# Eighteen loads of x behind the last store of an FFT and gated-cosine kernel

## The chip, the core and the metric

The kernel runs on one core of a Trainium2 chip. The metric is the time of one execution on the device in microseconds (us). TensorE (PE) multiplies matrices, VectorE (DVE), ScalarE (ACT) and GpSimd (POOL) work on elements, SyncE (SP) issues most DMAs, and 16 DMA engines move the data between DRAM and SBUF, the memory of 128 partitions on the core. A DMA that SP or ACT issues is split over these engines; it tells its end by a semaphore, on which whatever needs the data waits.

## The reference

Two stages. The first is the real part of a Fourier transform of x over sequence and channel; the second is a two-layer network with the gate h cos(h).

```
x: (8, 3008, 256) float32;  w_in: (256, 2048);  w_out: (2048, 256)
X = np.fft.fft(np.fft.fft(x, axis=1), axis=2).real.astype(np.float32)
x = X.reshape(24064, 256)
h = x @ w_in
g = h * np.cos(h)
out = (g @ w_out).astype(np.float32)
```

## The kernel before

The 3008 positions of a sequence are written as 47 x 64: `x_r` is x seen as (batch, s2, s1, channel) with 47 values of s2 and 64 of s1. One s2 is 64 rows of 1 KB that lie next to each other in DRAM, so that `x_r[b, r0:r0+k, i0:i1]` is k pieces of (i1 - i0) KB, 64 KB apart. The transform goes in two halves (`first_half`, `second_half`) with a turn through DRAM in between (`store_z`, `load_z`); the second stage takes the result in steps of 256 columns and two blocks of 128 hidden channels (`mm1`, `act_e`, `dve_h`, `act_round`, `dve_frac`, `act_sin`, `dve_g`, `dve_s`, `mm2`), and its results go out through `store_out`.

Two SBUF tiles of 128 partitions x 4096 floats, `xs[0]` and `xs[1]` (tile name `xp` in the profile), hold the part of x that is being worked on. For the first batch `load_x` fills them (line 194): rows s2 of 0 to 31 go to partitions 32, 34, ... 94, those of 31 to 46 to partitions 0, 2, ... 30, and the mirrored positions, read backwards, go to the odd partitions in the same places. The descriptors, one for each piece that a DMA engine moves, are cut to 1 KB by `max_dma_last_dim=1024`. For later batches `load_later_x` (line 180) loads them in groups of at most seven rows, and `fold_rows` on POOL (line 325) and `middle_later` on PE (line 350) read them.

Other loads and stores that the prediction uses: the first matrix in `load_w` (lines 226 and 232, 128 partitions, 2 KB pieces), the second in `load_w2` (line 244, two DMAs of 512 KB in 1 KB pieces one right after the other), the intermediate in `load_z` (line 511), and in `second_half` a row of 1 KB that SP stores to DRAM (line 545) and spreads back over the partitions with the next DMA (line 546), which reads what the first one wrote.

The order of the work is written by hand: `tc.manual_schedule()` keeps the instructions of each engine and each queue in the order of the calls, and the framework adds the semaphore waits that the reads and writes of the tiles ask for. A loop over the steps `t` calls every stage; in its last turn it calls `combine_last`, which forms the last results and stores them in two halves of four DMAs each with `store_last` (line 906), on SP, ACT and one on POOL, and then leaves the loop. Nothing follows but the closing of the program (line 1149 in the profile).

Of the kernel before, what the change touches and what calls it, by code (L numbers as in the profile page):

```python
# [18 lines left out]
ND = 256  # L19
# [115 lines left out]
def kernel(  # L135
# [930 lines left out]
    for t in range(LAG, n + LAG + 1):  # L1066
# [55 lines left out]
        for call in todo.pop(t, ()):  # L1122
            call[0](*call[1:])


# [1 line left out]
_INS = ['x', 'moe_w_in', 'moe_w_out']  # L1127
# [26 lines left out]
```

## Time and profile before

| | |
|---|---|
| median of 2 runs | 1933.53 us (1933.52 to 1933.53) |
| the profiled execution, its own time | 1935.07 us |
| its span, first to last instruction | 1933.3 us |
| mean granted TensorE clock | 0.998 |
| busy share of PE, DVE, ACT, POOL | 99%, 92%, 79%, 21% |
| moved by the DMA engines | 89.16 MB, a mean of 46 GB/s |
| last reads of `xs[0]` and `xs[1]` by POOL (line 325) | begin at 1623.3 us |
| last four stores on SP (line 906) | 1927.49 to 1930.09 us |

All times inside the execution are from the start of the span. The profile shows one execution; its own time is that of the same execution with what lies around the span. An engine's busy share counts its instructions, not the issuing of DMAs; what SP, ACT and POOL issue stands in rows marked with a q behind the engine (SPq) or with the operation DMA_DIRECT2D. The rows named DMA and GB/s cut a stretch of time into 40 equal slices: the first gives the mean busy share of the 16 DMA engines in tenths, the second what they moved.

### The profile page before, as it was taken

To read this page: it belongs to the slowest core of one execution; us is meant where nothing else is said; L and a number is where in the kernel's file an instruction comes from. 1 tells how busy PE (TensorE), PEld (TensorE's weight loads), DVE (VectorE), ACT (ScalarE), POOL (GpSimd) and SP (SyncE) were. 2 spreads that over 40 slices of the span, in tenths; PEclk is the share of its full clock that TensorE was granted. 3 is DMA by queue.
4 is the path that set the end of the run, shared out by engine and by line. 5 is a ranking of instruction groups with operands and counts; after the bars stand their busy time and mean duration, and the time that the engine had idled before them with its cause. 6 is when DMAs were issued, how large, how long until landed. Compare 5 with 4: busy or idle time off the path is not lost.

```text
span 1933.3 us, 30495 instructions
## 1 busy us (share of the span) xinstructions
PE 1919.4 (99%) x9520; PEld 1690.2 (87%) x9520; DVE 1778.9 (92%) x3338; ACT 1527.8 (79%) x2870; POOL 413.5 (21%) x494
## 2 busy tenths in 40 slices
PE   9999999999999999999999999999999999999998
PEld 5888899888998889988898888988889888898887
DVE  5999989999899998999989999999999999999998
ACT  4787888788788887888877887788877888788775
POOL 5322112221122211222112221122211222111111
PEclk9999999999999999999999999999999999999999
DMA  7311220012111121112211022110131000110000
GB/s 201 108 54 43 76 55 24 22 47 76 47 25 26 46 81 38 27 25 55 78 31 31 21 56 83 29 26 24 53 85 31 25 20 24 55 28 10 12 22 23
DMA packets 160215, 89.16 MB, mean 46 GB/s; under 512 B 108039, under 2 KB 154910, under 8 KB 157713
## 3 DMA queue, kind: packets, MB, share of 16 engines
q1 hardware_dynamic: 158653, 85.58, 16.6%
q8 instruction: 76, 1.25, 0.3%
q0 software_dynamic: 896, 1.07, 0.2%
q14 instruction: 86, 0.70, 0.1%
q10 hardware_dynamic: 504, 0.56, 0.1%
HBM read 49.88 MB, written 37.28 MB: 45 GB/s over the span
## 4 chain that ended last, share of the span: by engine, by line
PE 96%; DMA 2%; SPq 1%; DVE 1%; issue 0%; POOL 0%; ACT 0%; ACTq 0%; DVEq 0%; POOLq 0%
PE M L812 58%; PE H L721 33%; PE pb L525 2%; PE pz L419 2%; DMA w<-in_moe_w_out_dram 1%; DMA xp<-in_x_dram 1%; SPq L194 0%; POOL VX L864 0%; PE pz L453 0%; DMA zd<-zs 0%; PE pz L350 0%; PE M L419 0%; SPq L502 0%; DMA out_dram<-ob 0%; DMA xz<-in_x_dram 0%
## 5 line engine op out<-in xcount | busy, mean ns | idle before, releaser
L812 PE MATMUL M<-S,VX 128*128 128x256 f32 (+1 forms) x2304 | 612.6, 375 | 0.0
L812 PEld LDWEIGHTS M<-S,VX 128*128 128x128 f32 x2304 | 438.3, 190 | 49.4
L752 ACT ACTIVATE r<-H 128x512 f32<-128x512 f32 (+1 forms) x384 | 226.0, 589 | 262.9 <-DVE h L737 261.6
L762 ACT ACTIVATE r<-r 128x1024 f32<-128x1024 f32 (+1 forms) x384 | 394.8, 1028 | 21.3 <-DVE r L756 15.8
L721 PE MATMUL H<-pq,WC 128*128 128x256 f32 (+1 forms) x1536 | 393.8, 379 | 0.7 <-ACT H L691 0.7
L721 PE MATMUL H<-pq,WS 128*128 128x256 f32 (+1 forms) x1536 | 388.3, 375 | 1.7 <-ACT ew L732 1.5
L812 PE MATMUL M<-r,w 128*128 128x256 f32 (+1 forms) x1536 | 387.9, 375 | 0.0
L691 ACT ACTIVATE H<-nb,wn 128x256 f32<-128x256 f32 (+1 forms) x762 | 360.6, 473 | 16.2 <-DMA wn<-wd 2.4
L737 DVE TENSOR_TENSOR h<-ew,H 128x512 f32<-128x512 f32 (+1 forms) x384 | 258.6, 673 | 99.7 <-PE H L721 64.1
L721 PEld LDWEIGHTS H<-pq,WC 128*128 128x128 f32 x1536 | 283.7, 190 | 49.8 <-ACT r L752 16.2
L812 PEld LDWEIGHTS M<-r,w 128*128 128x128 f32 x1536 | 300.5, 196 | 27.1
L721 PEld LDWEIGHTS H<-pq,WS 128*128 128x128 f32 x1536 | 291.6, 190 | 36.0 <-ACT ew L732 3.2
L756 DVE SCALAR_TENSOR_TENSOR r<-r,H 128x512 f32<-128x512 f32 (+1 forms) x384 | 258.7, 674 | 25.4 <-ACT r L752 9.1
L864 POOL TENSOR_TENSOR cb<-cb,mr 128x256 f32<-128x256 f32 (+3 forms) x190 | 159.6, 850 | 523.1 <-DVE S L787 484.0
L732 ACT ACTIVATE ew<-H 128x512 f32<-128x512 f32 (+1 forms) x384 | 225.6, 587 | 54.3 <-PE H L721 45.4
L756 DVE SCALAR_TENSOR_TENSOR r<-r,h 128x512 f32<-128x512 f32 (+1 forms) x384 | 259.4, 675 | 0.0
L777 DVE TENSOR_TENSOR S<-r 128x512 f32<-128x512 f32 (+1 forms) x384 | 258.8, 674 | 0.1
L766 DVE SCALAR_TENSOR_TENSOR r<-h,r 128x512 f32<-128x512 f32 (+1 forms) x384 | 258.0, 672 | 0.0
L766 DVE SCALAR_TENSOR_TENSOR r<-H,r 128x512 f32<-128x512 f32 (+1 forms) x384 | 255.8, 666 | 2.3 <-ACT r L762 1.7
L752 ACT ACTIVATE r<-h 128x512 f32<-128x512 f32 (+1 forms) x384 | 235.9, 614 | 0.0
L812 PE MATMUL M<-S,w 128*128 128x256 f32 (+1 forms) x768 | 226.1, 376 | 1.5 <-DVE S L787 1.5
L325 POOL TENSOR_TENSOR xs<-xp 113x512 f32<-113x512 f32 x112 | 142.9, 1276 | 387.2 <-DVE S L787 387.2
(106 smaller groups left out, 1587.8 us busy)
## 6 DMA issues: line engine op xcount, KB each, us to landing
out_dram<-ob SPq DMA_DIRECT2D x726, 32.0 KB
xp<-in_x_dram SPq DMA_DIRECT2D x256, 56.0 KB
z<-zd SPq DMA_DIRECT2D x8, 1280.0 KB
zd<-zs SPq DMA_DIRECT2D x224, 40.0 KB
nb<-nd SPq DMA_DIRECT2D x39, 128.0 KB
zd<-zs SPq DMA_DIRECT2D x224, 8.0 KB
xp<-in_x_dram SPq DMA_DIRECT2D x52, 48.0 KB
xp<-in_x_dram SPq DMA_DIRECT2D x42, 49.0 KB
```

Source lines behind the costliest of these rows:

```text
L325: return nc.gpsimd.tensor_tensor(out=xs2[e][0:XL], in0=xv[:, 0], in1=xv[:, 1], op=ALU.subtract if e else ALU.add,)
L691: nc.scalar.activation(out=s.H[:, u * T : u * T + T], in_=s.nb[:, 0:T], func=AF.Copy, bias=0.25, scale=wn[:, f : f + 1],)
L721: nc.tensor.matmul(s.H[:, u * T : u * T + T], lhsT=W[:, 128 * f : 128 * f + 128], rhs=s.pq[:, e * T : e * T + T], start=False, stop=True, ...
L732: nc.scalar.mul(out=s.ew[:, 0 : 2 * s.T], in_=s.H[:, 0 : 2 * s.T], mul=2.0)
L737: return nc.vector.tensor_tensor(out=s.h[:, 0 : 2 * T].rearrange("p (u t) -> p u t", u=2)[:, :, ::-1], in0=s.ew[:, 0 : 2 * T].rearrange("p ...
L752: nc.scalar.activation(out=r, in_=h, func=AF.Copy, bias=BIG, scale=1.0)
L756: nc.vector.scalar_tensor_tensor(out=r, in0=r, scalar=-BIG, in1=h, op0=ALU.add, op1=ALU.subtract)
L762: nc.scalar.activation(out=r, in_=r, func=AF.Sin, bias=0.0, scale=SIN_SCALE)
L766: nc.vector.scalar_tensor_tensor(out=r, in0=h, scalar=-0.25, in1=r, op0=ALU.add, op1=ALU.mult)
L777: return nc.vector.tensor_tensor(out=sv[:, 0:2], in0=gv[:, 2:3].to_broadcast([128, 2, T]), in1=gv[:, 0:4:3], op=ALU.subtract,)
L812: nc.tensor.matmul(acc[key][m // 2][:, 256 * (m % 2) : 256 * (m % 2) + T], lhsT=w, rhs=a, start=first, stop=s.fp == 7, skip_group_check=True,)
L864: return nc.gpsimd.tensor_tensor(out=o, in0=a, in1=b, op=ALU.subtract if less else ALU.add)
```

## The change

Behind the loop, as the last calls of the kernel, stand DMAs that read parts of the input x (batches 1 and 2) into `xs[0]`, here named `probe`. No instruction reads them.

`tokens(pitch, size)` loads to all 128 partitions: partition p gets four rows of 1 KB from position `pitch * p` on, so that with pitch 4 the source is one piece of 512 KB and with pitch 16 pieces of 4 KB 16 KB apart. `rows(queue, p0, step, r0, k, i0, i1, size)` loads k rows of s2, 16 KB each, to the partitions p0, p0 + step, and so on; with i1 below i0 it takes the 16 positions backwards. `size` is the largest piece in bytes. All but the last call go to SP's queue; the last goes to ACT's.

```diff
+    probe = xs[0]
+
+    def rows(queue, p0, step, r0, k, i0, i1, size, to=probe):
+        n = abs(i1 - i0)
+        queue.dma_start(
+            out=to[p0 : p0 + step * k - step + 1 : step, 0 : ND * n].rearrange(
+                "r (i d) -> r i d", d=ND
+            ),
+            in_=x_r[1, r0 : r0 + k, slice(i0, i1, -1 if i1 < i0 else 1)],
+            max_dma_last_dim=size,
+        )
+
+    def tokens(pitch, size):
+        flat = x[2, 0 : 128 * pitch].rearrange("(p i) d -> p i d", i=pitch)
+        nc.sync.dma_start(
+            out=probe[:, 0 : 4 * ND].rearrange("p (i d) -> p i d", d=ND),
+            in_=flat[:, 0:4],
+            max_dma_last_dim=size,
+        )
+
+    sp, act = nc.sync, nc.scalar
+    tokens(4, 2048)
+    rows(sp, 32, 2, 0, 32, 0, 16, 1024)
+    rows(sp, 32, 2, 0, 32, 0, 16, 2048)
+    rows(sp, 32, 2, 0, 32, 0, 16, 8192)
+    rows(sp, 32, 2, 0, 32, 63, 47, 1024)
+    tokens(4, 2048)
+    tokens(16, 2048)
+    rows(sp, 0, 1, 0, 32, 0, 16, 1024)
+    rows(sp, 0, 4, 0, 32, 0, 16, 1024)
+    rows(sp, 32, 4, 0, 16, 0, 16, 1024)
+    rows(sp, 0, 1, 0, 16, 0, 16, 1024)
+    rows(sp, 0, 7, 0, 16, 0, 16, 1024)
+    for k in range(2):
+        rows(sp, 32, 2, 0, 32, 0, 16, 1024)
+        rows(sp, 33, 2, 0, 32, 63, 47, 1024)
+    rows(sp, 32, 2, 0, 32, 0, 16, 1024)
+    rows(act, 33, 2, 0, 32, 63, 47, 1024)
```

The text numbers the loads 1 to 18 in the order of these calls.

## The prediction

> **What bounds the kernel now.** I read the page first, then the end of the order of time on the engines, then the DMA rows of a few short stretches in which a load runs nearly by itself. The first lines say that TensorE sets the time from start to finish: it is busy 99% of the span, and the chain that ended last runs through the matmuls of lines 812 and 721.
>
> ```profile
> span 1933.3 us, 30495 instructions
> PE 1919.4 (99%) x9520; PEld 1690.2 (87%) x9520; DVE 1778.9 (92%) x3338; ACT 1527.8 (79%) x2870; POOL 413.5 (21%) x494
> PE 96%; DMA 2%; SPq 1%; DVE 1%; issue 0%; POOL 0%; ACT 0%; ACTq 0%; DVEq 0%; POOLq 0%
> ```
>
> None of that matters for work behind the last store: there nothing is left to hide under. What counts is the tail. The order of time for SP gives its last issues, and the view of who waited for whom on SP's queue gives the wait at the program's end (line 1149 is the closing of the program):
>
> ```profile
> 1928.75 1.34 SPq L906 DMA_DIRECT2D out_dram<-ob  x2
> ...
> SPq L1149 <- DMA out_dram<-ob: 1.8, 1, 1.8
> ```
>
> The last store is issued by 1930.09; the program then waits 1.8 us for the stores to land, to about 1931.9, and closes 1.4 us later at 1933.3. Whatever is appended starts at about 1930.1, and the closing moves with its last landing. Every microsecond of it after 1931.9 is paid in full.
>
> **What is added.** The diff issues 18 DMAs when it is counted out, 17 on SP and the last on ACT: three of 512 KB to all 128 partitions (`tokens`), twelve of 512 KB to 32 partitions and three of 256 KB to 16 partitions (`rows`). In all 15 x 0.524 + 3 x 0.262 = 8.65 MB. No engine computes, nothing is taken away, and nothing earlier moves, since the calls stand last on SP and ACT. The tile they write is read last by the folds on POOL at line 325, which end at 1624.6, so the first of them waits for nothing but its turn.
>
> **Who waits for whom.** A load that writes bytes of an earlier one must wait until that one has landed. Loads to interleaved rows need not: the twelve loads at line 194 go to even rows, odd rows and rows below 32 of one tile and are issued every 0.65 us without a wait, though they take far longer to land (the second line is of the chain that ended last: the twelfth is issued at 8.22 and has landed 9.94 us later).
>
> ```profile
> L194 SPq DMA_DIRECT2D xp<-in_x_dram x12: 609/612/772, 0.7 to 8.2; - x12
> ...
> 8.22 9.94 DMA xp<-in_x_dram
> ```
>
> So I go through the partitions. Loads 1 to 10 each overlap their predecessor and run one after the other. Load 11 (partitions 0 to 15) doesn't touch load 10 (32, 36, ... 92) and is issued right behind it. Load 12 (every seventh) meets both. The last six alternate between even and odd rows, so two are always in flight, and each waits for the one two before it. The chain has nine single steps, then 10 with 11, then 12, then three rounds of two.
>
> **The price of one step.** It has four pieces. *Hand-over*: a DMA that waits for another on the same queue starts almost at once. The 1 KB pair at lines 545 and 546 takes 283.26 to 284.35, so 1.09 us with everything in it; that is the floor of any step.
>
> ```profile
> 283.26 0.23 SPq L545 DMA_DIRECT2D nd<-pq  x1
> 284.35 0.35 SPq L546 DMA_DIRECT2D nb<-nd  x1
> ```
>
> *Issue to first packet*, from the DMA rows of two stretches. The 256 KB load of z is issued at 27.64; in the stretch 27.5 to 31 (slices of 0.0875 us) the first bytes come in the 13th slice, at 28.55: 0.9 us. The two 512 KB loads of w, cut into 1 KB pieces as most of the new loads are, are issued from 29.89; in the stretch 29.5 to 36 (slices of 0.1625 us) the stream begins at 31.6: 1.7 us.
>
> ```profile
> DMA  0000000000001568776635556400000000000009
> GB/s 0 0 0 0 0 0 0 0 0 0 0 0 70 211 234 328 304 234 187 257 141 187 211 211 234 164 24 0 0 0 0 0 23 0 0 0 0 0 0 70
> ...
> DMA  5400000069140269999999999999998677777777
> GB/s 202 151 0 0 13 0 0 0 25 76 50 25 0 57 195 347 397 384 365 384 391 384 460 347 365 359 372 340 359 347 284 208 205 199 205 214 224 218 218 217
> ```
>
> *Data.* With the queue full, the row loads of x run at 244 GB/s (6 to 18 us) and the 128-partition loads in 2 KB pieces at 404 (18 to 22); the w loads reach about 365. The lone z load needs some 1.2 us for its 262 KB, about 220 GB/s, because its engines don't start together. For 0.524 MB that is 1.3 us at 404, 1.45 at 365, 2.15 at 244.
>
> ```profile
> 6.00:18.00 12.00, 10.38 (x45) 4.45 (x43) 3.76 (x6) 1.59 (x5) 5.41 (x9) 1.00 1.03 244
> 18.00:22.00 4.00, 3.70 (x15) 1.97 (x17) 3.71 (x7) 1.94 (x6) 2.15 (x4) 0.66 1.06 404
> ```
>
> *Last packet to semaphore*: the last stores move until 1931.25 (DMA row of 1929 to 1934) and are waited for until 1931.9, 0.65 us; a load may need less, I take 0.5.
>
> **The sum.** A row load in 1 KB pieces: 1.7 + 1.85 (between 1.45 and 2.15) + 0.5 + 0.05 = 4.1. In 2 KB pieces 4.0, in 8 KB pieces 3.9, as fewer pieces should start sooner. A `tokens` load: 1.3 (between 0.9 and 1.7) + 1.55 + 0.55 = 3.4; the first 3.6, as stores are still moving; the one with gaps in the source 3.5. No row shows a load packed into rows 0 to 31, or into 0 to 15: bounds 3.8 and 6.5 (half the rate of 244), I take 5.0 for load 8 and 4.3 for load 9, which spreads over all rows. Loads 10 and 11: 0.65 until the second is issued + 2.25 + 1.7 for its data (0.7 to 2.15) = 4.6. Load 12: 3.6. The last six: with two in flight the start of one hides under the data of the other, so a round takes one step or two loads' data, 4.1 or 2 x 2.15; three rounds of 4.3 and 0.65 are 13.6.
>
> Loads 1 to 5: 3.6 + 4.1 + 4.0 + 3.9 + 4.1 = 19.7. 6 and 7: 6.9. 8 and 9: 9.3. 10 and 11: 4.6. 12: 3.6. 13 to 18: 13.6. Together 57.7, from 1930.1 on. The old wait of 1.8 goes under it, so the span grows by 55.9, from 1933.3 to 1989.2; the profiled execution, 1935.07 with what lies around its span, would show 1991. The median of the runs, 1933.53, is 1.5 lower, and with the same addition becomes **1989.4**.
>
> Bounds: with the z load's start (0.9 + 0.55) and 365 to 404 GB/s everywhere, 2.9 a row load and 2.8 a `tokens` load, the chain is 40.3, the time 1972. With 5.5 for each 512 KB step (the second w load took 6.38 from its issue behind the first), the chain is about 77, the time 2009.
>
> [...]
>
> **The rivals.**
> *Lean loads:* a single load starts as soon as z's did and moves at the full queue's rate; by the lower bound above 1972 to 1978. For it speaks the z row; against it 1.7 us to the first packet of the w loads, and z's own 220 GB/s. [...]
> *Loads that overlap:* no load waits for another. Then issues take 17 x 0.65 = 11 us and the queue's rate decides: 1.7 + 8.65 MB / 244 GB/s (35.4) + 0.5 = 37.6 from 1930.1, less 1.8: 1969. Against it stands the pair at 545 and 546, where a DMA waits for a DMA of its own queue.
> *Heavy loads:* one of the 16 engines lags in each load and every step takes 6 us or more, as 6.38 and 9.94 above hint, though those stood in a queue: 2010 to 2020.
> *Not slower:* the loads don't sit behind the stores. If they are dropped, or start once the tile is free at 1624.6, they run beside the matmuls, where the page's slices show DMA engines at most two tenths busy; 58 us fit into the 300 left, and the time stays 1933 to 1935. It decides as soon as the first load stands ahead of SP's last stores. Against it: SP's issues in the trace follow the order of the code line by line.
>
> **How the numbers follow.** The forecast as costed 0.76; lean loads 0.10, half of them above 1972.2; overlap 0.04; heavy 0.07; not slower 0.03. A change of 2%, about what a measurement of this kernel can tell from none, is 38.7 us, so the line is at 1972.2. Slower by more: 0.76 + 0.05 + 0.07 = 0.88. Within: 0.05 + 0.04 + 0.02 = 0.11. Faster: 0.01. The range runs from the lean loads to the upper bound, 1975 to 2010.
>
> **What would show it.** Busy times of PE, DVE, ACT and POOL are unchanged, and SP's issues up to 1930 keep their times. Behind it stand 17 issues on SP 3 to 5 us apart but for the close pairs; the DMA row shows a burst and a gap for each; the chain's DMA share rises from 2% to about 4 to 5%. The forecast is wrong if issues follow one another every 0.6 us, if single steps take under 3 us or over 5.5, or if loads appear before 1930.

## The result and the profile after

The change takes 1999.38 us against 1933.53: a ratio of 1.0341, 95% interval 1.0296 to 1.0385. It is slower, as forecast, and the time lies in the range, 10 us above the 1989.4 that were predicted.

The profiled execution took 1999.35 us, its span is 1997.6. First the lines of the page that answer to those of before:

```profile
span 1997.6 us, 30524 instructions
PE 1918.6 (96%) x9520; PEld 1688.5 (85%) x9520; DVE 1778.6 (89%) x3338; ACT 1528.1 (76%) x2870; POOL 413.9 (21%) x494
DMA  7311211022111130012210121102210001000025
PE 92%; DMA 2%; DVE 1%; SPq 1%; issue 0%; POOL 0%; ACT 0%; ACTq 0%; DVEq 0%; POOLq 0%
```

Busy times are those of before within 2 us; PE's share falls from 99% to 96% because the span is longer. What is new stands in the last slices: the DMA engines work there while the other engines stand still. One sign that the prediction named is not there: the share of DMA in the chain that ended last stays at 2%. The view of that chain has its last piece at 1927.08 us and doesn't follow the loads behind it, so it says nothing about them.

Next the order of time on SP's queue from the last store on: start, duration of the issue, line. Line 1139 is `tokens`, line 1129 `rows`, and the last of the 18 loads is on ACT's queue.

```profile
1928.24 0.88 SPq L906 DMA_DIRECT2D out_dram<-ob  x1
1929.23 0.54 SPq L1139 DMA_DIRECT2D xp<-in_x_dram  x1
1933.10 0.70 SPq L1129 DMA_DIRECT2D xp<-in_x_dram  x1
1938.18 0.65 SPq L1129 DMA_DIRECT2D xp<-in_x_dram  x1
1943.19 0.59 SPq L1129 DMA_DIRECT2D xp<-in_x_dram  x1
1948.27 0.59 SPq L1129 DMA_DIRECT2D xp<-in_x_dram  x1
1953.19 0.40 SPq L1139 DMA_DIRECT2D xp<-in_x_dram  x1
1956.70 0.37 SPq L1139 DMA_DIRECT2D xp<-in_x_dram  x1
1960.74 0.33 SPq L1129 DMA_DIRECT2D xp<-in_x_dram  x1
1965.50 0.63 SPq L1129 DMA_DIRECT2D xp<-in_x_dram  x1
1969.63 0.59 SPq L1129 DMA_DIRECT2D xp<-in_x_dram  x1
1970.26 0.60 SPq L1129 DMA_DIRECT2D xp<-in_x_dram  x1
1975.17 0.63 SPq L1129 DMA_DIRECT2D xp<-in_x_dram  x1
1978.60 0.62 SPq L1129 DMA_DIRECT2D xp<-in_x_dram  x1
1979.27 0.64 SPq L1129 DMA_DIRECT2D xp<-in_x_dram  x1
1983.74 0.59 SPq L1129 DMA_DIRECT2D xp<-in_x_dram  x1
1985.82 0.59 SPq L1129 DMA_DIRECT2D xp<-in_x_dram  x1
1988.69 0.59 SPq L1129 DMA_DIRECT2D xp<-in_x_dram  x1
...
1991.01 0.70 ACTq L1129 DMA_DIRECT2D xp<-in_x_dram  x1
```

Where a load waits for the one before it, the distance between two starts is the price of a step. The order of waits is the forecast one: only loads 11 (1970.26) and 14 (1979.27) follow their predecessor after 0.65 us; load 15 starts when 13 has landed, 16 when 14 has. The view of waits on SP's queue counts the same, 12 waits for 14 loads of `rows` and 2 for the later `tokens`:

```profile
SPq L1129 <- DMA xp<-in_x_dram: 42.3, 12, 4.4
SPq L1139 <- DMA xp<-in_x_dram: 7.3, 2, 4.2
SPq L1188 <- DMA xp<-in_x_dram: 6.9, 3, 2.8
```

The steps against the prediction's, in us; the last landing is at 1996.4 by the semaphores in the trace, and the program closes 1.2 us later:

| loads | predicted | measured | difference |
|---|---|---|---|
| 1, 6, 7 (128 partitions) | 10.5 | 3.87 + 3.51 + 4.04 = 11.4 | +0.9 |
| 2 to 5 (32, 34, ... 94) | 16.1 | 5.08 + 5.01 + 5.08 + 4.92 = 20.1 | +4.0 |
| 8, 9 | 9.3 | 4.76 + 4.13 = 8.9 | -0.4 |
| 10 with 11 | 4.6 | 5.54 | +0.9 |
| 12 | 3.6 | 3.43 | -0.2 |
| 13 to 18 | 13.6 | 17.8 | +4.2 |
| all | 57.7 | 67.1 | +9.4 |

The first load was issued at 1929.23, 0.9 us earlier than forecast (in the other runs with loads at this place it stands between 1926.5 and 1930.3), so the span is 8.4 us above the forecast 1989.2; the profiled execution of before was 1.5 us slower than its median, which makes up most of the rest to 10. Of the 9.4 us that the sum is short, 8.2 stand in the loads to every second partition from 32 or 33. Cutting into 1, 2 or 8 KB pieces (loads 2, 3, 4) makes no difference: 5.08, 5.01, 5.08. Load 9 reads the same bytes as load 2 in the same pieces and takes 4.13. What sets the price of such a load became the question. Three theories: **place** (the partitions written), **source** (rows 64 KB apart in DRAM) and **start** (the fixed part of a step was costed too low).

### The profile page after: what moved, and what is told of

Read it like the earlier page. It is cut to its first block, busy times and chain, and to the rows that moved or that the text cites. A ratio compares the mean times of both kernels' runs of the same rounds, so it can differ in the third digit from the quotient of the medians.

```text
span 1997.6 us, 30524 instructions
## 1 busy us (share of the span) xinstructions
PE 1918.6 (96%) x9520; PEld 1688.5 (85%) x9520; DVE 1778.6 (89%) x3338; ACT 1528.1 (76%) x2870; POOL 413.9 (21%) x494
## 2 busy tenths in 40 slices
DMA packets 167479, 97.81 MB, mean 49 GB/s; under 512 B 108327, under 2 KB 161086, under 8 KB 164913
## 4 chain that ended last, share of the span: by engine, by line
PE 92%; DMA 2%; DVE 1%; SPq 1%; issue 0%; POOL 0%; ACT 0%; ACTq 0%; DVEq 0%; POOLq 0%
PE M L812 56%; PE H L721 32%; PE pb L525 2%; PE pz L419 1%; DMA w<-in_moe_w_out_dram 1%; DMA xp<-in_x_dram 0%; SPq L194 0%; POOL VX L864 0%; DMA zd<-zs 0%; PE pz L350 0%; SPq L502 0%; PE M L419 0%; DMA xz<-in_x_dram 0%; DVE xf L312 0%; PE pz L407 0%
## 5 line engine op out<-in xcount | busy, mean ns | idle before, releaser
L812 PE MATMUL M<-r,VX 128*128 128x256 f32 (+1 forms) x768 | 225.0, 375 | 0.0
```

Source lines behind the costliest of these rows:

```text
L812: nc.tensor.matmul(acc[key][m // 2][:, 256 * (m % 2) : 256 * (m % 2) + T], lhsT=w, rhs=a, start=first, stop=s.fp == 7, skip_group_check=True,)
```

## The experiments

Experiments 1 to 4, 7 and 8 are read from one profiled execution each. How far a single step can be trusted shows in a load that stands alone in several runs: every fourth partition from 0 (1 KB pieces, rows 64 KB apart) took 4.08 to 4.23 us, partitions 32, 34, ... took 4.96 to 5.21.

**1. Ten places, one source.**

```diff
-    tokens(4, 2048)
-    ... (all 18 loads)
+    for p0, step in ((32, 2), (0, 4), (0, 1), (0, 2), (64, 2), (32, 1), (96, 1), (0, 3), (16, 2), (1, 4)):
+        tokens(4, 2048)
+        rows(sp, p0, step, 0, 32, 0, 16, 1024)
+    tokens(4, 2048)
```

> Ten row loads with one source (32 rows of 16 KB, 512 KB, 1 KB pieces) to ten sets of 32 partitions, each between two tokens loads, so that every load is alone and its step can be read from issue to next issue. Theory 'place' (the partitions that a load writes set its speed once it is under way): 5.1 us for partitions 32, 34, ..., 4.1 for every fourth partition from 0 or 1, 4.75 for 0 to 31, and about 5 for the others that are packed into 32 or 63 neighbours; every third partition lies between 4.1 and 4.6. Theory 'source' (rows 64 KB apart in DRAM) and theory 'start' (the fixed part of a step is longer than costed): all ten alike within 0.3 us, 4.1 to 5.1. [...]

The first two of the ten, with the `tokens` loads behind them:

```profile
1930.24 0.70 SPq L1129 DMA_DIRECT2D xp<-in_x_dram  x1
1935.36 0.40 SPq L1139 DMA_DIRECT2D xp<-in_x_dram  x1
1938.58 0.68 SPq L1129 DMA_DIRECT2D xp<-in_x_dram  x1
1942.67 0.38 SPq L1139 DMA_DIRECT2D xp<-in_x_dram  x1
```

The steps: (32, 2) 5.12, (0, 4) 4.09, (0, 1) 4.71, (0, 2) 5.22, (64, 2) 5.18, (32, 1) 4.81, (96, 1) 4.61, (0, 3) 4.82, (16, 2) 5.11, (1, 4) 3.92. Same bytes from the same rows, 1.3 us apart: the place decides. Every third partition, expected at 4.1 to 4.6, came with the packed ones. The DMA row of single steps shows how. Each of these two stretches is one step cut into 40 slices, the first for (32, 2), 0.128 us a slice, the second for (0, 4), 0.102 us:

```profile
GB/s 0 0 0 0 0 0 0 0 0 0 0 56 144 72 56 88 120 200 240 304 352 368 384 312 256 256 184 168 160 128 104 96 40 8 0 0 0 0 0 0
...
GB/s 0 0 0 0 0 0 0 0 0 0 0 0 0 0 40 90 110 40 110 120 240 250 230 200 300 280 391 381 351 411 351 431 331 251 140 70 10 0 0 0
```

Both start moving 1.4 us after the issue, both need 0.8 us to get going, both reach 350 to 430 GB/s. The spread load stays there until it ends; the packed one falls off after some 0.8 us near that rate and drags on. Its last bytes come 4.35 us after the issue, those of the spread one 3.8; then 0.8 us pass until the next issue where the load is packed, 0.3 where it is spread. The 0.8 us of the start, packed and then spread, with the rate last:

```profile
1931.60:1932.40 0.80, 0.00 (x0) 0.00 (x0) 0.00 (x0) 0.00 (x0) 0.00 (x0) 0.50 0.56 81
1939.90:1940.70 0.80, 0.00 (x0) 0.00 (x0) 0.00 (x0) 0.00 (x0) 0.00 (x0) 0.50 0.43 86
```

**2. Sizes.**

```diff
+    for p0, step in ((32, 2), (0, 4)):
+        for n in (1, 2, 4, 8, 16):
+            tokens(4, 2048)
+            rows(sp, p0, step, 0, 32, 0, n, 1024)
+    tokens(4, 2048)
```

> Row loads of 1, 2, 4, 8 and 16 KB a row (32 rows, 1 KB pieces), first to partitions 32, 34, ..., then to every fourth, each between two tokens loads. Theory 'place': both sets cost the same up to 8 KB a row (2.3, 2.4, 2.6 and 3.3 us), since a load's first microsecond runs at full speed, and part at 16 KB: 5.1 against 4.1. Theory 'start': the difference of 0.9 us is there at 1 KB a row already and doesn't grow. Theory 'source': no difference between the sets at any size.

With 1, 2, 4, 8 and 16 KB a row: 2.11, 2.33, 2.60, 3.36 and 5.21 for (32, 2); 1.98, 2.23, 2.48, 3.20 and 4.09 for (0, 4). Up to 8 KB a row (256 KB in all) the places differ by 0.10 to 0.16, no more than one load scatters from run to run; at 512 KB they differ by 1.12. That is the profile of experiment 1 in numbers: the second 256 KB cost 0.9 us where spread and 1.85 where packed. "Start" falls: a load of 32 rows costs 2.0 to 2.1 us at 1 KB a row in either place, less than the 2.25 (1.7 + 0.5 + 0.05) that the sum had for start and end.

**3. Sources.** `pitched(p0, step, pitch, size)` is `rows` with source rows `pitch` KB apart; a `tokens` load stands ahead of each.

```diff
+    for p0, step in ((0, 4), (32, 2)):
+        for pitch in (16, 17, 32, 64, 80):
+            tokens(4, 2048)
+            pitched(p0, step, pitch, 1024)
+    for size in (2048, 8192):
+        tokens(4, 2048)
+        pitched(0, 4, 64, size)
+    tokens(4, 2048)
+    rows(nc.sync, 0, 4, 0, 32, 63, 47, 1024)
+    tokens(4, 2048)
```

> The same 512 KB to every fourth partition and then to 32, 34, ..., from rows 16 KB apart (one contiguous piece), 17, 32, 64 and 80 KB apart; then every fourth partition in 2 KB and 8 KB pieces and with the positions backwards; a tokens load between any two. Theory 'place': 4.1 us for every fourth partition and 5.1 for 32, 34, ... whatever the distance, piece or direction, within 0.3. Theory 'source': at 64 KB the step is longer than at 16, 17 and 80 KB by 0.5 us or more in both sets. The prediction's own view of pieces would have 0.1 to 0.2 us less for 2 KB and 8 KB pieces.

Every fourth partition, 16 to 80 KB apart: 4.13, 3.96, 4.02, 4.09, 4.07. (32, 2): 4.71, 4.65, 4.87, 4.96, 5.02. In 2 and 8 KB pieces 4.02 and 3.85, backwards 4.22. "Source" falls as the cause: 64 KB is nothing special, and where the load is spread the distance does nothing. Packed, close rows save up to 0.37 and lie up to 0.45 under the 5.1, more than the 0.3 that "place" had allowed; why, is open. The prediction's view of pieces holds in part: 8 KB pieces to every fourth partition took 3.85 here and 3.98 and 3.74 in the two spread runs of experiment 6, under the 4.08 to 4.23 of 1 KB pieces; to 32, 34, ... the change shows nothing of it.

**4. Four in flight.**

```diff
+    for k in range(3):
+        rows(sp, 32, 2, 0, 32, 0, 16, 1024)
+        rows(sp, 33, 2, 0, 32, 0, 16, 1024)
+        rows(sp, 32, 2, 0, 32, 0, 16, 1024, xs[1])
+        rows(sp, 33, 2, 0, 32, 0, 16, 1024, xs[1])
+    tokens(4, 2048)
+    ... (the same from 0 and 2, every fourth partition)
```

> Twelve row loads of 512 KB with four places to go to (even and odd of 32 to 95 in both x tiles), so that four are in flight; then a tokens load; then twelve to every fourth partition from 0 and from 2 in both tiles; then a tokens load. Theory 'place': the packed set moves at some 200 GB/s, so its 6.3 MB take about 31 us from the first issue to the last landing; the spread set moves at about 380 GB/s and takes about 19 us. Theory 'start' (a step is waiting, and more loads in flight hide it): both sets take about 17 to 19 us, three rounds of 5 to 5.5 and the issues. The prediction's 244 GB/s for a full queue would give 28 us for both.

From first issue to last landing 29.9 us packed and 20.2 spread; "place" had said 31 and 19, the other two views the same time for both. The steady stretches, with the columns for busy engines empty, and the rate last:

```profile
1934.00:1952.00 18.00, 0.00 (x0) 0.00 (x0) 0.00 (x0) 0.00 (x0) 0.00 (x0) 0.50 1.11 237
1962.00:1976.00 14.00, 0.00 (x0) 0.00 (x0) 0.00 (x0) 0.00 (x0) 0.00 (x0) 0.50 1.06 360
```

The DMA engines are full in both (share 1.11 and 1.06), yet packed they move 237 GB/s: each piece takes longer. In the trace's DMA records, which have a time for each piece, one of 1 KB takes 75 ns at the median where packed and 46 where spread. 237 is near the 244 GB/s of the row loads at line 194, two thirds of whose bytes go to partitions 32 to 95: the prediction had a number near it and averaged it away.

**5. The loads inside the loop.** The 18 calls, unaltered, one in every second step from step 334 on, when the tile is free.

```diff
+    for k, call in enumerate(loads):
+        todo.setdefault(n - 50 + 2 * k, []).append(call)
```

> All 18 loads unaltered, but issued inside the loop, one in every second step from step 334 of 384 on (some 1680 us), after the last read of the tile. Theory of the prediction (the whole cost comes from standing behind the last store): 1933 to 1935, the same as before. Rival (the loads cost something wherever they stand, by holding up SP's stores and with them the output tiles, or by contending for the DMA engines): 1938 or more.

1933.09 us, a ratio of 1.0003 (0.9994 to 1.0012) to the kernel before. The page of its profile:

```profile
span 1932.4 us, 30520 instructions
DMA  7311220012111121112211022110121000132210
```

All 8.65 MB were moved (97.81 MB in all, as in the change), issued from 1690 to 1844 us beside busy engines, and cost nothing that the runs can tell. The whole price of the change is its position behind the last store.

**6. The mis-sized term taken out.** Loads 2 to 5 and 13 to 18 go to every fourth partition; all else is as in the change.

```diff
-    rows(sp, 32, 2, 0, 32, ...)
+    rows(sp, 0, 4, 0, 32, ...)
-    rows(act, 33, 2, 0, 32, 63, 47, 1024)
+    rows(act, 2, 4, 0, 32, 63, 47, 1024)
```

> The change with one thing altered: the ten 512 KB row loads that go to partitions 32, 34, ... or 33, 35, ... (loads 2 to 5 and 13 to 18) go to every fourth partition, from 0 or from 2. Same bytes, same sources, same number of loads, same order of waits. Theory 'place': loads 2 to 5 save 0.95 us each and the last six about 1 us a round and 0.5 at the start, 7 us in all: 1992. Theories 'source' and 'start': nothing changes, 1999 within 1 us.

It was measured a second time beside the change itself, on one chip:

> The change itself, timed beside the spread version on one chip. All theories: 1999 where the kernel before takes 1933, a ratio of 1.034.

> The spread version (ten row loads to every fourth partition) a second time, beside the change on the same chip. Theory 'place': 6 to 7 us less than the change, as the steps of the first profile of it have it (60.5 against 67.1 from the first issue to the last landing). Theories 'source' and 'start': no difference.

The first time 1993.58, ratio 1.0322 (1.0308 to 1.0336), with runs from 1990.7 to 1997.2; the second time 1991.54, ratio 1.0302 (1.0288 to 1.0316), beside 1998.15, ratio 1.0335 (1.0321 to 1.0349), for the change: 6.6 us less. The profiles agree: from first issue to last landing 60.5 and 60.2 us against 67.1 and 67.0. The spread run's queue:

```profile
1927.37 0.54 SPq L1139 DMA_DIRECT2D xp<-in_x_dram  x1
1931.03 12.51 SPq L1129 DMA_DIRECT2D xp<-in_x_dram  x4
1947.04 3.69 SPq L1139 DMA_DIRECT2D xp<-in_x_dram  x2
1954.43 26.67 SPq L1129 DMA_DIRECT2D xp<-in_x_dram  x10
```

Loads 2 to 5 now take 1947.04 - 1931.03 = 16.0 us, the predicted 16.1: 4.1 less than in the change, where "place" had said 3.8. The last six save 2.2 to 2.5, where it had said 3.5.

**7. Which partitions get in each other's way.** Sets of 16 partitions, as many rows as there are DMA engines (which engine takes which row, the trace doesn't say), four loads in flight to four tiles. The question is whether crowding of neighbours or the position sets the speed.

```diff
+    places = (xs[0], xs[1], VX, w2)
+    for p0, step in ((0, 8), (32, 4), (0, 4), (64, 4), (0, 7), (0, 2), (0, 1)):
+        for to in places:
+            whole(to)
+        for k in range(3):
+            for to in places:
+                rows(nc.sync, p0, step, 0, 16, 0, 16, 1024, to)
```

> Seven sets of 16 partitions, twelve row loads of 256 KB to each (3.15 MB, 1 KB pieces, one row a DMA engine), four in flight to four tiles that are no longer read; four loads to all partitions ahead of each set. [...]

The steady stretch of each set, in that order:

```profile
1938.00:1950.00 12.00, 0.00 (x0) 0.00 (x0) 0.00 (x0) 0.00 (x0) 0.00 (x0) 0.50 1.02 198
1958.00:1967.00 9.00, 0.00 (x0) 0.00 (x0) 0.00 (x0) 0.00 (x0) 0.00 (x0) 0.50 0.90 285
1976.00:1989.00 13.00, 0.00 (x0) 0.00 (x0) 0.00 (x0) 0.00 (x0) 0.00 (x0) 0.50 0.99 194
1999.00:2011.00 12.00, 0.00 (x0) 0.00 (x0) 0.00 (x0) 0.00 (x0) 0.00 (x0) 0.50 1.06 194
2020.00:2031.00 11.00, 0.00 (x0) 0.00 (x0) 0.00 (x0) 0.00 (x0) 0.00 (x0) 0.50 1.02 205
2040.00:2052.00 12.00, 0.00 (x0) 0.00 (x0) 0.00 (x0) 0.00 (x0) 0.00 (x0) 0.50 1.12 207
2062.00:2085.00 23.00, 0.00 (x0) 0.00 (x0) 0.00 (x0) 0.00 (x0) 0.00 (x0) 0.50 1.14 105
```

Every fourth partition from 32 to 92 runs at 285 GB/s, all of 0 to 15 at 105, the rest at about 200. Every eighth from 0 to 120, spread as widely as can be, is among the slow ones at 198, so wide spacing alone doesn't make a set fast. And with one and the same spacing the position counts: every fourth partition runs at 285 from 32, at 194 from 0 and from 64. From first issue to last landing the sets took 20.1, 15.4, 21.6, 20.4, 19.1, 19.7 and 35.2 us. The DMA records show it more sharply: a 1 KB piece takes 46 ns at the median in the fast set, 82 to 89 in those of every eighth, every second and every fourth from 0 and from 64, and 176 in 0 to 15; that 285 GB/s is less than twice the 198 is in part that the engines were not always busy there (share 0.90). Every seventh partition came to 205, with a median of 80 ns, and under a fifth of its pieces take less than 50. What it is in the position that makes a piece take 46, 85 or 176 ns was not shown.

**8. Twice the rows.** The same with sets of 32 partitions.

```diff
-    for p0, step in ((0, 8), (32, 4), (0, 4), (64, 4), (0, 7), (0, 2), (0, 1)):
+    for p0, step in ((0, 1), (0, 2), (32, 2), (0, 4)):
...
-                rows(nc.sync, p0, step, 0, 16, 0, 16, 1024, to)
+                rows(nc.sync, p0, step, 0, 32, 0, 16, 1024, to)
```

> Four sets of 32 partitions, twelve row loads of 512 KB to each (6.3 MB, two rows a DMA engine), four in flight to four tiles that are no longer read; four loads to all partitions ahead of each set. [...]

The steady stretch of each set, in the order of the diff:

```profile
1940.00:1962.00 22.00, 0.00 (x0) 0.00 (x0) 0.00 (x0) 0.00 (x0) 0.00 (x0) 0.50 1.12 201
1977.00:1999.00 22.00, 0.00 (x0) 0.00 (x0) 0.00 (x0) 0.00 (x0) 0.00 (x0) 0.50 1.12 201
2014.00:2031.00 17.00, 0.00 (x0) 0.00 (x0) 0.00 (x0) 0.00 (x0) 0.00 (x0) 0.50 1.12 250
2044.00:2056.00 12.00, 0.00 (x0) 0.00 (x0) 0.00 (x0) 0.00 (x0) 0.00 (x0) 0.50 1.08 378
```

The sets took 36.1, 36.6, 29.9 and 20.5 us. The pieces take 91 ns at the median in the first two sets, 72 in the third and 46 in the last. Beside experiment 7, all of 0 to 15 ran at 105 GB/s and 0 to 31 run at 201; every fourth partition ran at 194 from 0 to 60 and from 64 to 124, and both together run at 378; but every second ran at 207 with 16 partitions and runs at 201 with 32. So neither the spacing nor the number of partitions alone gives the rate. Why 32, 34, ... 94 comes to 250 and not 378 GB/s, stays open.

## Why the prediction was right, and where its sum was off

*Right: slower, and by what mechanism.* Everything behind the last store was paid in full; experiment 5 took the loads away from that place and the cost with them. The rival "not slower" described that very version, 1933 to 1935, and fell only because the change doesn't put them there.

*Right: who waits for whom.* Nine single steps, a pair, load 12 and three rounds of two are all in the order of time. "Loads that overlap" (1969) falls with the 12 and 2 waits of SP's queue. "Lean loads" (1972 to 1978) and "heavy loads" (2010 and more) fall with single steps of 3.4 to 5.1 us.

*Off: the step of a row load.* The step was 1.7 + 1.85 + 0.5 + 0.05 = 4.1. The 1.7 was misread from the row of the w loads: that row already shows 25 to 76 GB/s from 30.8 to 31.45 us (in the trace they are 1 KB pieces from 30.95 on), so the first bytes came about 1 us after the issue, and a slow beginning followed. In the two row loads of experiment 1 the first bytes come after 1.4 us, and 0.8 us at 81 and 86 GB/s follow. For a spread load the start, the slow beginning and the full rate make up 4.1 again, so that value was right there by errors that cancel. For partitions 32, 34, ... the step is 5.0. Experiment 1 shows where the added microsecond lies: a little over half of it in the data, which end at 4.35 us and not at 3.8, and the rest behind the last bytes, 0.8 us where the sum had 0.55. For the data I took the middle between 365 GB/s (128 partitions) and 244 (mostly these very partitions); the nearer row was the second, but with its 2.15 the step would still have been only 4.4. That is +4.0 for loads 2 to 5, and experiment 6 gave it back.

*Off: the last six.* A round was costed at 4.3, a start hidden under the partner's data. In the trace a packed load with a partner takes 5.0 to 5.3, about what it takes alone, the very first odd one 6.5; a round is set by the same step. Spread, the six still took 15.3 to 15.6 us against 13.6, so a little over half of the 4.2 is the place. The rest stays when the place is taken out: the spread loads of the later chain (14, 16, 18) take 4.8 to 5.2 where one alone takes 4.1, so a round lies above the 4.3 even there. Why a partner makes a load longer was not tried.

*Off: loads 10 and 11.* Load 11 writes partitions 0 to 15, which experiment 7 shows at 105 GB/s. At that rate 0.262 MB take 2.5 us, not the 1.7 of the sum, which would be most of the +0.9; load 11 was not run alone.

*Not explained:* by what the partitions written set the rate, of which experiments 1, 7 and 8 show the size alone. Nor why load 7, with gaps in its source, takes 4.04 where load 6 takes 3.51; the other runs with all 18 loads at this place show 0.7 to 0.8 us more. Load 7 was not tried apart.

## What to carry to other kernels

What stood behind the last store of this kernel cost its full time: 18 loads that are free beside the matmuls cost 66 us there. Here a load of 32 rows that waits for another cost 2.0 us at 32 KB and 4 to 5 at 512 KB (the 1 KB pair at lines 545 and 546 took 1.09), so such a chain is priced by its steps as much as by its bytes. For a load to part of the partitions take the rate from a row with the same partitions; spreading 32 rows over every fourth partition was worth 1 us in 5.

## What the runs showed of the hardware that I had not expected

A lone load of 32 rows isn't at its rate when it starts moving: about 0.8 us at 85 GB/s come first (experiment 1: 81 and 86). To partitions 32, 34, ... the first 256 KB take about as long as to every fourth, the second take 1.85 us against 0.9 (experiment 2: 3.36 against 3.20 us at 256 KB, 5.21 against 4.09 at 512); whether bytes in all or bytes a row decide, was not separated. For a lone 512 KB load to every fourth partition the distance of the source rows from 16 to 80 KB does nothing clear, and 8 KB pieces saved 0.1 to 0.4 us on 1 KB ones in the same run. And wide spacing alone doesn't make a load fast: every eighth partition took 198 GB/s where every fourth from 32 took 285, and a 1 KB piece 85 ns where it took 46.
